# A layer-norm, linear-attention and gated-FFN block: apply order, folded query weights, and the first FFN handover

## The chip, the cores and the metric

The kernel runs on one core of a Trainium2 chip. The time is device microseconds from one launch; the median of 12 runs is compared. A core has five engines that work from queues of their own and wait for each other through semaphores: TensorE (PE, matmuls; PEld is its weight load), VectorE (DVE), ScalarE (ACT), GpSimd (POOL) and SyncE (SP, which here only issues DMAs).

## The reference, cut to what matters

With S = 2048 rows, D = 640, H = 32 heads of Dh = 20, FF = 1536, all in bfloat16:

```python
def _A_ref(x, wqkv, w_phi, wo):                     # x is layernorm(A_x)
    qkv = (x @ wqkv).reshape(B, S, 3, H, Dh)...     # q, k, v per head
    pq, pk = q @ w_phi[h], k @ w_phi[h]             # per head, Dh x Dh
    phi_q = concat([softmax(pq), softmax(-pq)])
    phi_k = concat([softmax(pk), softmax(-pk)])
    kv, z = phi_k^T v, sum_s phi_k                  # over all rows
    o = (phi_q kv) / (phi_q z + 1e-6)
    return o.reshape(B, S, D) @ wo
def _B_ref(x, w_gate, w_up, w_down):
    return (gelu(x @ w_gate) * (x @ w_up)) @ w_down
h  = x + _A_ref(layernorm(x), ...)
h2 = h + _B_ref(layernorm(h), ...)
```

## The kernel before, in words

The rows are cut into NT = 16 tiles of 128 rows, in NB = 4 blocks of four tiles; D is NC = 5 chunks of 128. All five engines run in the order in which the program issues their instructions: the whole body stands under a manual schedule, so nothing is reordered, and an instruction that waits holds everything behind it on its engine.

**Stage 1, the k/v loop.** `w_phi` is folded into the key and query weights (`fold`, L203): for each of five row chunks d, six matmuls into one PSUM tile `wa`, copied to `Wk2` or `Wq2` by ACT (L212, even d) or DVE (L214, odd d). Layer norm of a tile has two steps. `ln_st` takes the statistics of two tiles at a time: on DVE `stats` (L101) and `mv` (L102), on POOL `ve` (L104), `rstd` (L106) and `mr` (L111). `ln_ap` applies them on ACT (L117), and SP issues a DMA transpose into `LN1T` (L133); the first six tiles use TensorE transposes instead. The loop over t = 0 to 15 does `k_tile(t)` (ten matmuls L239 into `pk`, and two exponentials `E` on ACT, L262), `v_tile(t+3)` (ten matmuls into `pv`, and a copy `vS` on ACT, L250), `ln_ap(t+5)`, at odd t `ln_st(t+7, t+8)`, then `k_norm(t)` and, at odd t from 5 on, `kv_tile(t-5)` and `kv_tile(t-4)` (40 matmuls together, L284). `k_norm` is on DVE a sum per head `sk` (L268) and a reciprocal `rs` (L270), and then two products `vt` (L273): one half always on POOL, the other on POOL for odd t up to 11 and on DVE otherwise. At t = 1 POOL also fills `KV` and `kmask` (L353 to L361). At t = 12 the whole query fold runs, ahead of `v_tile(15)`. At t = 10 SP issues the loads of `Wo` and `Wu`.

**Stage 2, the query features.** There are 20 chunks (4 blocks by 5 chunks of D). `q_mm(j)` computes chunks 2j and 2j+1 into one PSUM tile `pq` (ten matmuls of 512 columns, L307), and `q_exp(j)` takes exp of both signs on ACT into `Eq[j]` (L312). Groups 0 to 3 run after t = 15 and ahead of the last `kv_tile`s (tiles 12 to 15) and of `kv_mask`, which makes `KV`; groups 4 to 9 are laid between the attention steps of tiles 0 and 1.

**Stage 3, attention, and handover to the FFN.** Per tile: `attn_a` (20 matmuls into two PSUM tiles `ab`, and two copies to `AB`, L412), `attn_b`, `b2`, `b3` (products, reciprocal, `tt` L441, `o` L445), a transpose into `oT`, `attn_c` (ten matmuls `po`, L460), `attn_d` (residual add L469 and statistics), `attn_e` (apply and transpose into `LN2T`). For tiles 0 and 1 the sequence is written out by hand. The FFN then starts with `gate_up` on columns 0 to 256 of block 0 (L500; `g` on ACT L503, `GT` on DVE L506), and `weave` lays the other tiles' attention steps between FFN units by position numbers.

**PSUM.** `gtile` hands out tiles of two banks in rotation: three of them in stages 1 and 2 (`psG`; `kvp` has the other two banks), four from group 4 on (`psG2`). A matmul that opens a tile waits until the tile handed out three (or four) requests ago has been read. So the order of the requests decides which ACT or DVE instruction a matmul waits for:

```python
psG = ps_cm.enter_context(tc.tile_pool(name="psG", bufs=3, space=PSUM, reuse_waits="tile"))
psG = ctx.enter_context(tc.tile_pool(name="psG2", bufs=4, space=PSUM, reuse_waits="tile"))
```

Of the kernel before, what the change touches and what calls it, by code (L numbers as in the profile page):

```python
# [8 lines left out]
BF16 = mybir.dt.bfloat16  # L9
F32 = mybir.dt.float32  # L10
ALU = mybir.AluOpType
ACTF = mybir.ActivationFunctionType
# [5 lines left out]
def kernel(  # L18
# [12 lines left out]
    nc = tc.nc  # L31
    P = 128
# [5 lines left out]
    NT = S // P  # L38
# [7 lines left out]
    NH = [(P * c + P - 1) // Dh - H0[c] + 1 for c in range(NC)]  # L46
    NWARM = 10
    VP = (1, 3, 5, 7, 9, 11)
    QT = (15, 15, 15, 15)
    VC = Dh + 1  # L50
    KC = Dh + 2
# [22 lines left out]
    Wu = const.tile([P, NC, FF], BF16, name="Wu")  # L74
    KV = const.tile([P, NC, 2, 4, KC], BF16, name="KV")

    Eq = [const.tile([P, 2, 2, 512], BF16, name=f"Eq{j}") for j in range(NB * NC // 2)]
    ident = const.tile([P, P], BF16, name="ident")
    hmask = const.tile([P, NC, 8], BF16, name="hmask")
    kmask = const.tile([P, NC, 4], BF16, name="kmask")  # L80
# [1 line left out]
    nhalf = const.tile([P, 2], F32, name="nhalf")  # L82

    def eq(t, c, s):
        j = t // 4 * NC + c
        return Eq[j // 2][:, j % 2, s, t % 4 * P:(t % 4 + 1) * P]

    def small(pool, shape, name, bufs=3):
        return pool.tile(shape, F32, name=name, bufs=bufs)
# [1 line left out]
    def gtile(name):  # L91
        return psG.tile([P, 2, 512], F32, name=name, tag="G")
# [93 lines left out]

    warm(NWARM)

    def fold(WT, W2, halves):


        runs = []
        for c in range(NC):
            lo, hi = H0[c] * Dh, (H0[c] + NH[c]) * Dh
            for u in range(2):
                a, b = max(lo, u * HD), min(hi, (u + 1) * HD)
                if a < b:
                    runs.append((u, c, a, b))
        runs.sort()
        for d in range(NC):  # L200
            wa = gtile("wa")
            for i, (u, c, a, b) in enumerate(runs):
                nc.tensor.matmul(wa[:, u, a - u * HD:b - u * HD], lhsT=WT[:, c, d * P:(d + 1) * P],  # L203
                                 rhs=BD[:, c].rearrange("p a b -> p (a b)")[:, a - H0[c] * Dh:b - H0[c] * Dh],
                                 start=(i == 0 or runs[i - 1][0] != u),
                                 stop=(i + 1 == len(runs) or runs[i + 1][0] != u), skip_group_check=True)
            dst, src = W2[:, d, :].rearrange("p (u f) -> p u f", u=2), wa[:, :, 0:HD]
            if halves:
                dst = W2[:, d, :].rearrange("p (c u f) -> p u c f", c=NC, u=2)
                src = src.rearrange("p u (c f) -> p u c f", c=NC)  # L210
            if d % 2 == 0:
                nc.scalar.copy(dst, src)  # L212
            else:
                nc.vector.tensor_copy(dst, src)  # L214
# [3 lines left out]
    def ln_st(*tiles, act=True):  # L218
        for t, v in zip(tiles, ln_stats(p1, [x_sb[t // 4][:, t % 4, :] for t in tiles], "1", act)):
            lnp[t] = v  # L220

    def ln_ap(t, on_act=False, on_pe=False):
        ln = (ln_act if on_act else ln_dve)(p1, "1", *lnp[t])
        if on_pe:
            lnp[t] = ln
        else:
            transpose_to(LN1T[t // 4][:, :, t % 4 * P:(t % 4 + 1) * P], ln, False)

    def ln_tp(t):
        transpose_to(LN1T[t // 4][:, :, t % 4 * P:(t % 4 + 1) * P], lnp[t], True)  # L230
# [22 lines left out]
    def v_tile(t):  # L253
        v_mm(t)
        v_ev(t)

    def k_tile(t):
        pk = gtile("pk")
        proj(pk, t, Wk2)
        Ek[t] = ev.tile([P, 2, D], BF16, name="E", bufs=8)  # L260
        for s in range(2):
            nc.scalar.activation(Ek[t][:, s, :].rearrange("p (u f) -> p u f", u=2), pk[:, :, 0:HD],  # L262
                                 ACTF.Exp, scale=(1.0 if s == 0 else -1.0))

    def k_norm(t):

        sk = small(p1, [P, 2 * H], "sk")
        nc.vector.reduce_sum(sk, Ek[t].rearrange("p s (h f) -> p (s h) f", f=Dh), axis=AX.X)  # L268
        rs = small(p1, [P, 2 * H], "rs")
        nc.vector.reciprocal(rs, sk)  # L270
        vt = ev.tile([P, 2, H, VC], BF16, name="vt", bufs=8)
        for s, eng in ((1, nc.gpsimd), (0, nc.gpsimd if t in VP else nc.vector)):
            eng.tensor_tensor(vt[:, s], vS[t % 6], rs[:, s * H:(s + 1) * H, None].to_broadcast([P, H, VC]), ALU.mult)  # L273
        Vt[t] = vt
# [3 lines left out]
    def kv_tile(t):  # L278

        for s in range(2):  # L280
            for c in range(NC):
                for u in range(2):
                    f0, h0 = u * HD + c * 64, u * UH + 3 * c
                    nc.tensor.matmul(kvp[HALF[u], s, c * 4 * VC:(c + 1) * 4 * VC],  # L284
                                     lhsT=Ek[t][:, s, f0:f0 + 64], rhs=Vt[t][:, s, h0:h0 + 4, :],
                                     start=(c == 0 and t == 0), stop=(t == NT - 1), skip_group_check=True)
# [10 lines left out]

    pqs = {}

    def q_mm(j, i=None):  # L300

        if i != 1:
            pqs[j] = gtile("pq")
        for i in range(2) if i is None else (i,):
            b, c = divmod(2 * j + i, NC)
            for kc in range(NC):
                nc.tensor.matmul(pqs[j][:, i, :], lhsT=Wq2[:, kc, c * P:(c + 1) * P], rhs=LN1T[b][:, kc, :],  # L307
                                 start=(kc == 0), stop=(kc == NC - 1))

    def q_exp(j, signs=(0, 1)):  # L310
        for s in signs:
            nc.scalar.activation(Eq[j][:, :, s, :], pqs[j], ACTF.Exp, scale=(1.0, -1.0)[s])  # L312

    ln_st(0, act=False)
    ln_st(1, act=False)
# [26 lines left out]
    ev = ev_cm.__enter__()  # L342

    for t in range(NT):
        k_tile(t)
        if t == 0:
            ln_ap(4, on_pe=True)
            ln_tp(4)
            ln_ap(5, on_pe=True)
            ln_st(6, 7)  # L350
        if t == 1:
            ln_tp(5)
            nc.gpsimd.memset(KV, 0.0)  # L353
            nc.gpsimd.memset(kmask, 1.0)
            for r in HALF:
                nc.gpsimd.affine_select(out=kmask[r], in_=kmask[r], pattern=[[4, NC], [-Dh, 4]],
                                        compare_op=ALU.is_ge, fill=0.0, base=0, channel_multiplier=1)
                nc.gpsimd.affine_select(out=kmask[r], in_=kmask[r], pattern=[[-4, NC], [Dh, 4]],
                                        compare_op=ALU.is_ge, fill=0.0, base=Dh - 1, channel_multiplier=-1)
            nc.gpsimd.tensor_copy(KV[:, :, 0, :, KC - 1], kmask)  # L360
            nc.gpsimd.tensor_copy(KV[:, :, 1, :, 0], kmask)  # L361
        if t == 12:
            fold(WqT, Wq2, True)
        if t + 3 < NT:
            v_tile(t + 3)
        if 6 <= t + 5 < NT:
            ln_ap(t + 5, on_act=True)
        if t % 2 == 1 and t + 7 < NT:
            ln_st(t + 7, t + 8)
        k_norm(t)  # L370
        if t % 2 == 1 and t >= 5:
            kv_tile(t - 5)
            kv_tile(t - 4)
        if t == 10:
            nc.sync.dma_start(Wo, wo_v)
            nc.sync.dma_start(Wu, wu_v)
        for j in range(len(QT)):
            if t == QT[j]:
                q_mm(j)
                q_exp(j)  # L380
# [14 lines left out]

    LN2T, st = {}, {}

    def attn_a(t, dve=False):

        b = t // 4  # L400
        if b not in LN2T:
            LN2T[b] = p2.tile([P, NC, 512], BF16, name="LN2T", bufs=2)
        AB = p2r.tile([P, 2, H, KC], F32, name="AB", bufs=2)
        ab = gtile("ab"), gtile("ab")
        for s in range(2):
            for c in range(NC):
                for u, r in enumerate(HALF):
                    nc.tensor.matmul(ab[u][:, s, 3 * c * KC:(3 * c + 4) * KC], lhsT=eq(t, c, s)[r],  # L408
                                     rhs=KV[r, c, s].rearrange("p h f -> p (h f)"),
                                     start=(c == 0), stop=(c == NC - 1), skip_group_check=True)  # L410
        for u in range(2):
            (nc.vector.tensor_copy if dve and u == 1 else nc.scalar.copy)(  # L412
                AB[:, :, u * UH:(u + 1) * UH].rearrange("p s h f -> p s (h f)"), ab[u][:, :, 0:UH * KC])
        st[t] = AB

    def attn_b(t, on_pe=False):

# [59 lines left out]
    def attn_d2(t):  # L477
# [10 lines left out]
        nc.gpsimd.tensor_scalar(v[:, 2:3], sm[:, 0:1], rstd, -1.0 / D, op0=ALU.mult, op1=ALU.mult)  # L488
        st[t] = ht, None, rstd, v[:, 2:3]

    def attn_e(t, on_pe=False, on_dve=False):
        ln = (ln_dve if on_pe else ln_act)(p2, "2", *st[t])
        transpose_to(LN2T[t // 4][:, :, t % 4 * P:(t % 4 + 1) * P], ln, on_pe, on_dve)

    def gate_up(b, f, a0, a1):
# [58 lines left out]


    q_mm(q)
    attn_a(0, True)
    q_exp(q)
    q_mm(q + 1)
    attn_b(0, True)  # L560
    attn_b2(0, True)
    attn_b3(0, True)
    attn_a(1, True)
    q_exp(q + 1)
    q_mm(q + 2)
    attn_t(0)
# [8 lines left out]
    attn_t(1)  # L575
    q_exp(q + 3, (1,))
    q_mm(q + 4)
    attn_c(1)
    q_exp(q + 4)
    q_mm(q + 5, 0)  # L580
    attn_e(0, True)
    attn_d(1, False)
    q_mm(q + 5, 1)
    q_exp(q + 5)
    attn_a(2)
    attn_e(1, True, True)
    assert q + 6 == len(Eq)

    def attn_at(t, i, offs):

# [48 lines left out]
```

## Time and profile before

| what | value |
|---|---|
| median of 12 runs | 289.67 us (288.59 to 290.19) |
| the profiled execution's own time | 288.59 us |
| its span, first to last instruction | 286.9 us, so 1.7 us lie around it |
| TensorE busy | 274.0 us (96%), granted clock 0.999 |
| TensorE weight load busy | 172.2 us (60%) |
| DVE, ACT, POOL busy | 167.9, 143.8, 98.0 us |

Busy shares of TensorE count pipelined matmuls, whose ends are modelled, so a row of ten projections shows 1.52 us but follows the row before it after 1.36 us. Times within the span are starts in microseconds from its beginning. In a row of the timeline the first number is the start, the second the length; the bracket at the end is how long the engine had been idle before, and what ended that.

### The profile page before, as it was taken

What the parts mean: (1) busy time and instruction counts of PE and PEld (TensorE: products, weight loads), DVE (VectorE), ACT (ScalarE), POOL (GpSimd) and SP (SyncE); (2) the same over time, 40 slices, a digit from 0 to 9 for tenths busy, and PEclk for the clock granted to TensorE, in tenths of its full rate; (3) what the DMA queues carried; (4) which work ended last, traced back from release to release, by engine and by line L of the source; (5) the groups of instructions that cost most, each with busy time, mean ns of one, the idle gap of its engine ahead of it and who ended that gap; (6) DMA issues with size and microseconds to landing.
All of it is one profiled execution on the core that took longest, in us unless ns stands there. A gap on an engine that the chain in (4) does not pass through costs nothing.

```text
span 286.9 us, 5742 instructions
## 1 busy us (share of the span) xinstructions
PE 274.0 (96%) x2314; PEld 172.2 (60%) x2329; DVE 167.9 (59%) x284; ACT 143.8 (50%) x228; POOL 98.0 (34%) x209
## 2 busy tenths in 40 slices
PE   7899899979999899999999999999999999999995
PEld 2676577755545577777874454676455567444573
DVE  6789999989268466675623657532485732323322
ACT  2578788665968867536425445332445441132200
POOL 6239977866210223643420246220124340000000
PEclk9999999999999999999999999999999999999999
DMA  7997422390080011323311112232021323000011
GB/s 229 250 341 214 49 47 49 61 375 4 2 276 0 0 20 30 56 62 70 69 30 42 23 23 49 47 66 73 0 44 23 52 46 93 25 1 0 0 48 46
DMA packets 40971, 21.05 MB, mean 73 GB/s; under 512 B 33136, under 2 KB 39280, under 8 KB 40944
## 3 DMA queue, kind: packets, MB, share of 16 engines
q1 hardware_dynamic: 39856, 19.67, 27.2%
q10 hardware_dynamic: 1088, 1.01, 1.1%
q8 instruction: 18, 0.29, 0.4%
q14 instruction: 9, 0.07, 0.1%
HBM read 10.18 MB, written 2.62 MB: 45 GB/s over the span
## 4 chain that ended last, share of the span: by engine, by line
PE 74%; DVE 15%; DMA 3%; ACT 3%; issue 1%; POOL 1%; SPq 0%; DVEq 0%; ACTq 0%; POOLq 0%
PE gu L500 34%; PE pd L515 18%; PE pq L307 8%; PE po L460 7%; DVE sk L268 6%; DVE vt L273 3%; DMA Wv<-in_A_wqkv_dram 2%; DVE rs L270 2%; PE ab L408 2%; DVE stats L101 2%; PE pk L239 2%; PE pv L239 2%; ACT Eq L312 1%; DMA oT<-o 1%; PE kvp L284 1%
## 5 line engine op out<-in xcount | busy, mean ns | idle before, releaser
L503 ACT ACTIVATE g<-gu 128x512 bf16<-128x512 f32 (+1 forms) x60 | 30.7, 512 | 73.5 <-PE gu L500 72.7
L506 DVE TENSOR_TENSOR GT<-gu,g 128x512 bf16<-128x512 f32 (+1 forms) x60 | 34.5, 581 | 55.9 <-ACT g L503 55.8
L500 PE MATMUL gu<-LN2T,Wg 128*128 128x512 bf16 (+1 forms) x289 | 61.3, 335 | 2.0 <-DVE GT L506 0.8
L500 PE MATMUL gu<-LN2T,Wu 128*128 128x512 bf16 (+1 forms) x300 | 61.7, 336 | 0.0
L515 PE MATMUL pd<-Wd,GT 128*128 128x320 bf16 x384 | 53.9, 299 | 0.0
L515 PEld LDWEIGHTS <-GT 128*128 128x128 bf16 x384 | 37.4, 98 | 15.7 <-DVE GT L506 0.9
L500 PEld LDWEIGHTS <-Wu 128*128 128x128 bf16 x300 | 29.4, 98 | 22.6
L500 PEld LDWEIGHTS <-Wg 128*128 128x128 bf16 x300 | 28.4, 98 | 22.3 <-issue 1.7
L239 PEld LDWEIGHTS <-LN1T 128*128 128x128 bf16 x320 | 30.5, 98 | 15.6 <-DMA LN1T<-ln 2.7
L273 POOL TENSOR_TENSOR vt<-vS,rs 128x672 bf16<-128x672 bf16 x22 | 34.5, 1591 | 8.9 <-DVE rs L270 7.3
L521 DVE TENSOR_TENSOR y<-pd,x_sb 128x640 bf16<-128x640 f32 (+1 forms) x17 | 13.3, 784 | 30.7 <-PE pd L515 30.7
L412 ACT COPY AB<-ab 128x704 f32<-128x704 f32 x30 | 21.0, 749 | 14.8 <-PE ab L408 14.5
L239 PE MATMUL pv<-Wv,LN1T 128*128 128x320 bf16 x160 | 24.2, 299 | 2.6 <-DMA LN1T<-ln 2.1
L460 PE MATMUL po<-Wo,oT 128*128 128x320 bf16 x160 | 24.4, 299 | 0.2 <-DMA oT<-o 0.2
L239 PE MATMUL pk<-Wk,LN1T 128*128 128x320 bf16 x160 | 24.2, 299 | 0.3 <-DVE Wk L214 0.3
L441 DVE TENSOR_TENSOR tt<-AB,w 128x1280 bf16<-128x1280 f32 x16 | 23.8, 1486 | 1.2 <-POOL w L434 0.9
L262 ACT ACTIVATE E<-pk 128x640 bf16<-128x640 f32 x32 | 20.7, 702 | 7.1 <-PE pk L239 7.0
L268 DVE TENSOR_REDUCE sk<-E 128x64 f32<-128x1280 bf16 x16 | 23.2, 1452 | 0.8 <-ACT E L262 0.8
L307 PE MATMUL pq<-LN1T,Wq 128*128 128x512 bf16 x96 | 22.7, 379 | 0.6 <-ACT Eq L312 0.4
L312 ACT ACTIVATE Eq<-pq 128x1024 bf16<-128x1024 f32 x20 | 19.4, 1025 | 3.4 <-PE pq L307 3.4
L460 PEld LDWEIGHTS <-oT 128*128 128x128 bf16 x160 | 15.5, 98 | 7.6 <-DMA oT<-o 0.6
L483 POOL TENSOR_SCALAR v<-sm 128x1 f32<-128x1 f32 x14 | 8.4, 602 | 30.3 <-DVE x_sb L474 30.3
(77 smaller groups left out, 259.1 us busy)
## 6 DMA issues: line engine op xcount, KB each, us to landing
out_dram<-y SPq DMA_DIRECT2D x15, 160.0 KB, 1.8
Wg<-in_B_w_gate_dram SPq DMA_DIRECT2D x1, 1920.0 KB, 10.9
Wu<-in_B_w_up_dram SPq DMA_DIRECT2D x1, 1920.0 KB, 9.5
Wd<-in_B_w_down_dram SPq DMA_DIRECT2D x1, 1920.0 KB, 7.9
x_sb<-in_A_x_dram SPq DMA_DIRECT2D x2, 640.0 KB, 5.8
Wv<-in_A_wqkv_dram SPq DMA_DIRECT2D x2, 400.0 KB, 7.2
Wo<-in_A_wo_dram SPq DMA_DIRECT2D x1, 800.0 KB, 5.3
x_sb<-in_A_x_dram ACTq DMA_DIRECT2D x1, 640.0 KB, 7.3
```

What stands on the lines that cost most here:

```text
L239: nc.tensor.matmul(ps[:, u, 0:HD], lhsT=lnT(t, c), rhs=W[:, c, u * HD:(u + 1) * HD], start=(c == 0), stop=(c == NC - 1))
L268: nc.vector.reduce_sum(sk, Ek[t].rearrange("p s (h f) -> p (s h) f", f=Dh), axis=AX.X)
L273: eng.tensor_tensor(vt[:, s], vS[t % 6], rs[:, s * H:(s + 1) * H, None].to_broadcast([P, H, VC]), ALU.mult)
L307: nc.tensor.matmul(pqs[j][:, i, :], lhsT=Wq2[:, kc, c * P:(c + 1) * P], rhs=LN1T[b][:, kc, :], start=(kc == 0), stop=(kc == NC - 1))
L312: nc.scalar.activation(Eq[j][:, :, s, :], pqs[j], ACTF.Exp, scale=(1.0, -1.0)[s])
L412: (nc.vector.tensor_copy if dve and u == 1 else nc.scalar.copy)(AB[:, :, u * UH:(u + 1) * UH].rearrange("p s h f -> p s (h f)"), ab[u][:, ...
L441: nc.vector.tensor_tensor(tt.rearrange("p s (h f) -> p s h f", f=Dh), num, w[:, :, :, None].to_broadcast([P, 2, H, Dh]), ALU.mult)
L460: nc.tensor.matmul(po[:, u, 0:HD], lhsT=st[t][:, c, :], rhs=Wo[:, c, u * HD:(u + 1) * HD], start=(c == 0), stop=(c == NC - 1))
L500: nc.tensor.matmul(gu[:, i, 0:n], lhsT=W[:, c, f * P:(f + 1) * P], rhs=LN2T[b][:, c, a0:a1], start=(c == 0), stop=(c == NC - 1))
L503: nc.scalar.activation(g[:, 0:n], gu[:, 0, 0:n], ACTF.Gelu_apprx_tanh)
L506: nc.vector.tensor_tensor(st[b, "g", f][:, a0:a1], gu[:, 1, 0:n], g[:, 0:n], ALU.mult)
L515: nc.tensor.matmul(pd[:, u, 0:HD], lhsT=st[b, "g", f][:, tl * P:(tl + 1) * P], rhs=Wd[:, f, u * HD:(u + 1) * HD], start=(f == 0), stop=(f ...
```

## The change

Three places in the program are edited.

1. In the k/v loop `ln_ap(t+5)` is issued ahead of `k_tile(t)` instead of after `v_tile(t+3)`. The query fold is cut into its five pieces, one each at t = 8 to 12, after `v_tile` and ahead of `k_norm`. POOL's filling of `KV` and `kmask` goes from t = 1 to the end of t = 9.
2. The query chunks are grouped by the table `QG`: eleven groups in place of ten, of two chunks but for chunks 6 and 15, which stand alone. The four groups ahead of the last `kv_tile`s hold 7 chunks instead of 8; 13 follow.
3. In the hand-written sequence for tiles 0 and 1, `attn_e` is split so that the apply (`attn_ln`) can stand apart from the transpose. The last groups are not cut in halves any more, the copy of tile 0's `LN2T` goes from ACT to DVE, and `attn_a(2)` goes behind tile 1's transpose, with both its copies on DVE instead of ACT.

```diff
+    FQ = (8, 9, 10, 11, 12)
+    QG = ((0, 1), (2, 3), (4, 5), (6,), (7, 8), (9, 10), (11, 12), (13, 14), (15,), (16, 17), (18, 19))
...
-    Eq = [const.tile([P, 2, 2, 512], BF16, name=f"Eq{j}") for j in range(NB * NC // 2)]
+    Eq = [const.tile([P, len(g), 2, 512], BF16, name=f"Eq{j}") for j, g in enumerate(QG)]
...
-    def fold(WT, W2, halves):
+    def fold(WT, W2, halves, ds=range(NC)):
...
-        for d in range(NC):
+        for d in ds:
...
+    def q_mm(j):
+        pqs[j] = gtile("pq")
+        for i, bc in enumerate(QG[j]):
+            b, c = divmod(bc, NC)
...
-            nc.scalar.activation(Eq[j][:, :, s, :], pqs[j], ACTF.Exp, scale=(1.0, -1.0)[s])
+            nc.scalar.activation(Eq[j][:, :, s, :], pqs[j][:, 0:len(QG[j])], ACTF.Exp, scale=(1.0, -1.0)[s])
...
     for t in range(NT):
+        if 6 <= t + 5 < NT:
+            ln_ap(t + 5, on_act=True)
         k_tile(t)
...
         if t == 1:
             ln_tp(5)
+        if t + 3 < NT:
+            v_tile(t + 3)
+        if t % 2 == 1 and t + 7 < NT:
+            ln_st(t + 7, t + 8)
+        if t in FQ:
+            fold(WqT, Wq2, True, [FQ.index(t)])
+        k_norm(t)
+        if t % 2 == 1 and t >= 5:
+            kv_tile(t - 5)
+            kv_tile(t - 4)
+        if t == 9:
             nc.gpsimd.memset(KV, 0.0)
             nc.gpsimd.memset(kmask, 1.0)
...
-        if t == 12:
-            fold(WqT, Wq2, True)
-        if t + 3 < NT:
-            v_tile(t + 3)
-        if 6 <= t + 5 < NT:
-            ln_ap(t + 5, on_act=True)
-        if t % 2 == 1 and t + 7 < NT:
-            ln_st(t + 7, t + 8)
-        k_norm(t)
-        if t % 2 == 1 and t >= 5:
-            kv_tile(t - 5)
-            kv_tile(t - 4)
...
-    def attn_a(t, dve=False):
+    def attn_a_mm(t):
...
+    def attn_a_ev(t, dve=0):
+        AB, ab = st[t]
         for u in range(2):
-            (nc.vector.tensor_copy if dve and u == 1 else nc.scalar.copy)(
+            (nc.vector.tensor_copy if u >= 2 - dve else nc.scalar.copy)(
                 AB[:, :, u * UH:(u + 1) * UH].rearrange("p s h f -> p s (h f)"), ab[u][:, :, 0:UH * KC])
...
+    def attn_a(t, dve=0):
+        attn_a_mm(t)
+        attn_a_ev(t, dve)
...
+    def attn_ln(t, on_pe=False):
+        st[t] = (ln_dve if on_pe else ln_act)(p2, "2", *st[t])
+
     def attn_e(t, on_pe=False, on_dve=False):
-        ln = (ln_dve if on_pe else ln_act)(p2, "2", *st[t])
+        if not on_pe:
+            attn_ln(t)
+        ln = st[t]
...
     q_mm(q + 4)
+    q_exp(q + 4)
     attn_c(1)
-    q_exp(q + 4)
-    q_mm(q + 5, 0)
-    attn_e(0, True)
+    q_mm(q + 5)
+    q_exp(q + 5)
+    attn_ln(0, True)
     attn_d(1, False)
-    q_mm(q + 5, 1)
-    q_exp(q + 5)
-    attn_a(2)
+    attn_e(0, True, True)
+    q_mm(q + 6)
+    q_exp(q + 6)
+    attn_ln(1, True)
     attn_e(1, True, True)
-    assert q + 6 == len(Eq)
+    attn_a(2, 2)
+    assert q + 7 == len(Eq)
```

More of the change, by code (lines that the diff above doesn't have):

```diff
@@ L84, in eq @@
     def eq(t, c, s):
-        j = t // 4 * NC + c
-        return Eq[j // 2][:, j % 2, s, t % 4 * P:(t % 4 + 1) * P]
+        for E, g in zip(Eq, QG):
+            if t // 4 * NC + c in g:
+                return E[:, g.index(t // 4 * NC + c), s, t % 4 * P:(t % 4 + 1) * P]
     def small(pool, shape, name, bufs=3):
@@ L298 @@
     pqs = {}
[L300 to L305, printed above, removed]
+    def q_mm(j):
+        pqs[j] = gtile("pq")
+        for i, bc in enumerate(QG[j]):
+            b, c = divmod(bc, NC)
             for kc in range(NC):
@@ L410, in attn_a @@
                                      start=(c == 0), stop=(c == NC - 1), skip_group_check=True)
+        st[t] = AB, ab
+    def attn_a_ev(t, dve=0):
+        AB, ab = st[t]
         for u in range(2):
-            (nc.vector.tensor_copy if dve and u == 1 else nc.scalar.copy)(
+            (nc.vector.tensor_copy if u >= 2 - dve else nc.scalar.copy)(
                 AB[:, :, u * UH:(u + 1) * UH].rearrange("p s h f -> p s (h f)"), ab[u][:, :, 0:UH * KC])
         st[t] = AB
+    def attn_a(t, dve=0):
+        attn_a_mm(t)
+        attn_a_ev(t, dve)
     def attn_b(t, on_pe=False):
@@ L556 @@
     q_mm(q)
-    attn_a(0, True)
+    attn_a(0, 1)
     q_exp(q)
@@ L562 @@
     attn_b3(0, True)
-    attn_a(1, True)
+    attn_a(1, 1)
     q_exp(q + 1)
```

## The prediction, made before the changed kernel was run

> **What bounds the kernel now.** I read the engine shares, the chain that ended last, the timeline of TensorE (PE) for its gaps, and then the timeline of all engines around each gap.
>
> ```profile
> PE 274.0 (96%) x2314; PEld 172.2 (60%) x2329; DVE 167.9 (59%) x284; ACT 143.8 (50%) x228; POOL 98.0 (34%) x209
> PEclk9999999999999999999999999999999999999999
> ...
> PE 74%; DVE 15%; DMA 3%; ACT 3%; issue 1%; POOL 1%; SPq 0%; DVEq 0%; ACTq 0%; POOLq 0%
> ```
>
> PE is busy 96% of the span at full granted clock, and 74% of the chain is PE; the other large part is DVE (15%), all of it before 60 us. On the Trainium skill, "Perfetto Trace Analysis", Identifying the Most-Contended Engine, matmul busy time is a poor measure of headroom and weight-load busy time a good one. By it (60%) 40% of the span, some 115 us, would be open. The rows speak otherwise: ten projections follow each other in 1.36 us, forty `pq` matmuls in 8.66 us (67.98 to 76.64), without a gap between. I go by the gaps, which is all that an order can win:
>
> ```profile
> 26.93 1.53 PE L239 MATMUL pv<-Wv,LN1T 128*128 128x320 bf16 x10 [0.65 <-DMA LN1T<-ln]
> ...
> 33.94 1.53 PE L239 MATMUL pv<-Wv,LN1T 128*128 128x320 bf16 x10 [1.40 <-DMA LN1T<-ln]
> ...
> 58.48 0.47 PE L203 MATMUL wa<-BD,WqT 128*128 128x140 bf16 x6 [0.76 <-ACT E L262]
> ...
> 59.05 0.76 DVE L214 CAST Wq<-wa 128x640 bf16<-128x640 f32 x1
> ...
> 59.87 0.79 PE L203 MATMUL wa<-BD,WqT 128*128 128x140 bf16 x12 [0.91 <-DVE Wq L214]
> ...
> 97.94 0.45 PE L130 MATMUL tp<-ident,ln 128*128 128x128 bf16 x5 [0.62 <-DVE ln L122]
> ...
> 98.97 0.71 PE L500 MATMUL gu<-LN2T,Wg 128*128 128x256 bf16 x5 [0.58 <-DVE LN2T L131]
> ```
>
> The bracket is the idle time. PE waits for a transposed tile (`LN1T`) at 26.9 and 33.9 us; from the end of the matmuls before, this is 0.81 and 1.57 us (24.76 + 1.36 and 31.01 + 1.36 to the next start). The query fold waits for `E` and for its DVE copies (0.75 and 0.92 us): the copies at 59.05 stand on DVE behind the `k_norm`s. Group 4 waits 0.38 us for `Eq`. At the handover PE idles 0.62, 0.58 and 0.37 us (at 97.9, 99.0, 102.3). That is 6 us in all, 4.4 of it ahead of attention. From 102.3 us on there are only 0.5 us (130.4) and 0.4 us (141.9).
>
> ```profile
> 38.56 0.21 DVE L102 BATCH_NORM_AGGREGATE mv<-stats 128x2 f32<-128x12 f32 x1
> ...
> 39.98 0.50 POOL L111 TENSOR_SCALAR mr<-mv,rstd 128x1 f32<-128x1 f32 x2
> ...
> 40.69 1.29 ACT L262 ACTIVATE E<-pk 128x640 bf16<-128x640 f32 x2
> ...
> 42.57 0.92 ACT L117 ACTIVATE ln<-x_sb,mr,rstd 128x640 bf16<-128x640 bf16 x1
> ...
> 47.41 0.50 POOL L111 TENSOR_SCALAR mr<-mv,rstd 128x1 f32<-128x1 f32 x2
> ...
> 50.31 1.28 DVE L273 TENSOR_TENSOR vt<-vS,rs 128x672 bf16<-128x672 bf16 x1
> ```
>
> The third view is the cover of the change's first step: what the apply needs. At t = 7 the statistics end on DVE at 38.77, POOL gives `mr` at 40.2, `E` of t = 7 starts on ACT at 40.69, and the apply only at 42.57. So the apply never waits for `mr` today. DVE has hardly a gap from 18.9 to 51.6 us (the timeline lists none above 0.2 us); `mr` cannot come earlier.
>
> **The change part by part.** I walk the queues with the trace's spacings: projection 1.36 us; fold piece 0.40 (0.79 for two at 56.9); pair of `kv_tile`s 0.98 (41.74 to 42.72); query chunk 1.08 (8.66/8); on ACT apply to `E` 0.82, two `E` 1.30, `E` to `vS` 1.19, `vS` to the next 0.59; `Wq` copy 0.69 on ACT, 0.79 on DVE.
>
> *Apply ahead of `k_tile`.* Same instructions; the SP order of transposes, and of `Wo`/`Wu` behind them, is unchanged. The apply of tile 6 runs at 20.3 instead of 22.95 and its transpose lands before 25 (3.0 us later; 3.9 for tile 8), so both `LN1T` waits go. The price is that `E(t)` stands behind the apply. At t = 1 this costs PE 0.4 us (E ends 22.4, `pk(2)` needs its buffer). Then pv(8) starts at 32.0 instead of 33.94. Moving POOL's filling away lets `mr` of tiles 8 and 9 come at 25.6 instead of 27.26, in time.
>
> *The new wait.* At t = 5, 7, 9 the apply waits for `mr` of the statistics two steps back: 32.8, 40.2, 47.7 us by the rows. Behind it on ACT are `E(t)`, `vS` and, from t = 8, a `Wq` copy; on them wait `pk`/`pv` through the three PSUM tiles. The walk: t = 5, hidden (PE reaches its next need of that tile at 35.7, E ends 35.0). t = 7: E ends 42.4, pv(11) could open at 42.1: 0.3 us. From t = 8 the fold piece takes one request in three, so `pk(t+1)` opens the tile that `E(t)` has to free: `pk(9)` waits 0.8 us (E(8) ends 44.97), `pk(10)` 0.7 us (E(9) ends 49.84). Nothing in the trace shows this wait. Below it is 0 (if ACT or PE arrive later than walked, the wait is already paid); above, 0.82 plus 1.30 us for each of the three, 6.4 us. I take the walk's 1.9, since every term is a row; both ends are kept.
>
> *Fold in pieces.* The PE work (2.0 us) and five copies stay; the waits of 0.75 and 0.92 us go. DVE's two copies now sit after `vt(8)` (ends 51.6, so 52.4) and after `vt(10)` (58.7); the pieces that need their tiles come at 52.6 and 59.85: 0.2 and 1.2 us of cover. If DVE were late, PE would stall one for one.
>
> *POOL filling.* 2.5 us (23.02 to 25.54) go behind `vt(9)`, to 57.5 to 60. Behind it are `vt(10)` and `vt(11)`, done by 64.5; `kv_tile`(10, 11) asks at 65.3: covered by 0.8 us. A rule speaks against this: the Trainium skill, "SBUF — State Buffer", SBUF: two separate sides, has DVE operations with two inputs and POOL exclude each other for a whole instruction. The rows with a collision show DVE's `vt` at 1.35 instead of 0.86 us. At t = 1 the filling slowed nothing on DVE (`sk` 1.43 there and elsewhere); at its new place it meets `vt(10)` at most. By the row 0, by the rule 0.5 us on DVE, inside the 1.2 us of cover: 0 on the sum either way.
>
> *Seven chunks ahead of KV.* PE then runs pk(12) at 57.1, pv(15), fold, pk(13), kv at 61.6, pk(14), pk(15), kv at 65.3, queries from 66.3 to 73.8, last `kv_tile`s to 75.5. DVE, later by two copies and earlier by its old gaps, ends `vt(15)` at 73.1 and POOL's half at 74.2; tile 15 is asked for at 75.1: covered. Group 4 waits for the one-chunk exponentials (not in the trace: between half of 1025 ns and 597 ns, the FFN's 128x512 row; I take 0.55) until 75.9. `attn_a(0)` starts at 78.2 instead of 80.99: 2.8 us, less the 1.08 us of the chunk put off, **1.7 us won**.
>
> *Handover.* In the old frame: `pq` of one chunk ends at 91.95 instead of 93.02, but `attn_c(1)` opens the tile of group 7, whose second exponential ends at 92.51 (it stands behind the `oT` copy): 0.55 us of new idling. Then group 9, transpose 0, group 10 (to 98.6), transpose 1, `attn_a(2)`, 99.4. The first FFN unit needs `LN2T` (99.5) and the tile of group 10, so its exponentials, 98.7 to 100.65. The activation table load (1.28 us) now follows at once instead of after ACT's two `AB` copies, which move to DVE (0.89 instead of 0.75 us each; idle there, GT waits 2.9 us today). First `g` at 101.95 for 101.40, third FFN unit at 103.4. Less the chunk, 102.3 against 102.29: **0**. The waits inside this stage are from -0.6 us (no idling at `attn_c(1)`) to +0.6 us.
>
> Sum: -1.7 us and 0. Against the profiled execution's own 288.59 us (span 286.9) that is 286.9 us; that run is the lowest of the twelve, 1.1 us under the median, so against the median 289.67 it is **287.9 us**.
>
> One more rule weighs on the new stalls: the Trainium skill, "TensorE: Matmul & The Clock Gate", A second HAM failure mode, has short idles between groups that rotate through PSUM drop the clock. Here the granted clock is 9 of 10 or more in all 40 slices, after stalls of 0.81 and 1.57 us too, so I charge 0. By the rule, a half clock over the 8 us of matmuls between 42 and 50 us would cost 4 us at most (an estimate), and the sum turns to +2.3.
>
> **The rivals.**
> (a) *The new wait costs nothing*: PE's stalls at t = 7 to 9 do not appear. For it: each is only 0.3 to 0.8 us, of spacing errors added over 20 us. Against it: `mr` is paced by DVE, which is full. Then -1.7 - 1.9 = -3.6, 286.1 us.
> (b) *The loop wins, the handover gives back*: `attn_c(1)` and the first FFN unit idle by 0.6 us more each. For it: both wait for ACT, which is 4.97 of 5 us busy between 85 and 90. -0.5, 289.2 us.
> (c) *Slower: the statistics pace the loop.* The place is the apply at t = 5, 7 and 9; the price is up to 2.1 us each. The edit wins 0.81 + 1.57 + 0.75 + 0.92 = 4.05 us of old waits less 0.4 at t = 1; it turns slower once the three waits take over 3.6 us together, 1.2 each. With 1.5 each it is +0.9, 290.6 us. Against: POOL had been idle 0.95 us ahead of each `ve`.
> (d) That the change does not do what it says: the orders are the program's own, so I give it nothing.
>
> **How the numbers follow.** The walk 0.57 (own range 287.0 to 288.8), (a) 0.21, (b) 0.15, (c) 0.07. Changes within 0.2% (0.58 us) are about what a measurement of this kernel cannot tell from none. Faster: 0.57 + 0.21 + nearly half of (b) = 0.85; same 0.08; slower 0.07. The range 285.9 to 289.6 takes in the walk, (a) and most of (b), and leaves (c) out.
>
> **What would show it.** Right: no PE wait on `LN1T`; `pv(8)` near 32 us; ACT idling for POOL's `mr` ahead of the applies of tiles 10, 12, 14; PE waiting on ACT's `E` at 42 to 50 us; no wait on `Wq`; first `ab` matmul near 78.2; then `po` waiting about 0.5 us on `Eq`, and the first `gu` on the last `Eq`. Wrong: `wa` waiting on DVE, `kvp` waiting on `vt`, or a granted clock under 0.99.

## The result, and the profile after

The changed kernel takes 286.13 us (median of 8 runs, 285.38 to 287.14) against 289.55 us before (32 runs); the ratio is 0.9882, 95% interval 0.9864 to 0.9901. It is faster by 3.4 us, twice the 1.7 us of the walk and close to what rival (a) had, though not for its reason.

The two profiled executions must be compared with care. That of before (288.59 us) was the fastest of its first twelve; that of the changed kernel took 287.22 us, more than all eight other runs of it. In the changed kernel's profile the start was late, ahead of all edited code: TensorE waited 1.1 us for `Wv` and 0.8 us for the key weights' transpose `WkT` (before: 0.6 us and nothing), and the first `pk` matmul started at 17.42 us instead of 16.05. So stretches are counted from the first `pk`; the rows shown keep the start that the profile gives. From the page of the changed kernel, engine shares, clock row and chain:

```profile
PE 273.5 (96%) x2314; PEld 172.1 (60%) x2329; DVE 170.6 (60%) x287; ACT 141.7 (50%) x227; POOL 97.2 (34%) x209
...
PEclk9999999999999999999999999999999999999999
...
PE 77%; DVE 9%; DMA 6%; ACT 3%; POOL 2%; issue 2%; DVEq 0%; ACTq 0%; POOLq 0%
```

Shares and clock are as they were; in the chain DVE fell from 15% to 9%, PE rose from 74% to 77%. The rows of the timeline of TensorE and ACT that answer to the gaps shown of before (the bracket is the idle time ahead of the row's first instruction):

```profile
17.42 1.52 PE L243 MATMUL pk<-Wk,LN1T 128*128 128x320 bf16 x10 [0.18 <-DVE Wk L218]
...
28.75 1.53 PE L243 MATMUL pv<-Wv,LN1T 128*128 128x320 bf16 x10 [0.73 <-DMA LN1T<-ln]
...
34.19 1.52 PE L243 MATMUL pv<-Wv,LN1T 128*128 128x320 bf16 x10
...
46.55 1.52 PE L243 MATMUL pk<-Wk,LN1T 128*128 128x320 bf16 x10 [0.39 <-ACT E L266]
...
49.30 0.92 ACT L121 ACTIVATE ln<-x_sb,mr,rstd 128x640 bf16<-128x640 bf16 x1 [1.62 <-POOL mr L115]
...
51.46 1.52 PE L243 MATMUL pk<-Wk,LN1T 128*128 128x320 bf16 x10 [0.83 <-ACT E L266]
...
54.17 0.48 PE L207 MATMUL wa<-BD,WqT 128*128 128x140 bf16 x6
...
61.23 0.48 PE L207 MATMUL wa<-BD,WqT 128*128 128x140 bf16 x6
```

None of the five fold pieces has a bracket, the two shown and the three others: no wait for DVE's copies is left. The wait at pv(8), 1.40 us before, is gone, but that at pv(6) is still there. Two waits for `E` are new (0.39 and 0.83 us; a third, 0.21 us at pk(2), is the price at t = 1, walked at 0.4). The ACT row shows what is behind the second, an apply that keeps ACT waiting 1.62 us for `mr`. The same kernel at the handover, all engines:

```profile
79.17 0.57 PE L412 MATMUL ab<-KV,Eq 64*128 64x88 bf16 x20
...
88.79 0.83 DVE L481 TENSOR_TENSOR x_sb<-po,x_sb 128x640 bf16<-128x640 f32 x1 [0.37 <-PE po L472]
...
89.66 2.01 ACT L315 ACTIVATE Eq<-pq 128x1024 bf16<-128x1024 f32 x3
...
89.95 1.52 PE L472 MATMUL po<-Wo,oT 128*128 128x320 bf16 x10
...
95.90 0.44 PE L134 MATMUL tp<-ident,ln 128*128 128x128 bf16 x5
96.10 1.94 ACT L315 ACTIVATE Eq<-pq 128x1024 bf16<-128x1024 f32 x2 [0.50 <-PE pq L310]
...
96.39 0.49 DVE L135 COPY LN2T<-tp 128x640 bf16<-128x640 bf16 x1 [0.71 <-PE tp L134]
...
96.88 1.69 DVE L420 COPY AB<-ab 128x704 f32<-128x704 f32 x2
96.93 0.71 PE L517 MATMUL gu<-LN2T,Wg 128*128 128x256 bf16 x5
...
98.06 1.28 ACT L520 ACT_TABLE_LOAD   x1
...
100.25 0.71 PE L517 MATMUL gu<-LN2T,Wg 128*128 128x256 bf16 x5 [0.37 <-DVE GT L523]
```

`po` of tile 1 and the first `gu` have no bracket either: they start at 89.95 and 96.93 while ACT is still working on exponentials that the prediction had them wait for (to 90.7 and to 98.0 us; the row at 89.66 holds group 7's second exponential, which takes 1.03 us, and the two of group 8). The same three places in the timeline of before:

```profile
16.05 1.52 PE L239 MATMUL pk<-Wk,LN1T 128*128 128x320 bf16 x10 [0.29 <-DVE Wk L214]
...
80.99 0.56 PE L408 MATMUL ab<-KV,Eq 64*128 64x88 bf16 x20
...
102.29 0.71 PE L500 MATMUL gu<-LN2T,Wg 128*128 128x256 bf16 x5 [0.37 <-DVE GT L506]
```

This table, from these rows, splits the gain:

| | first pk to first ab | less a chunk (1.08) put off | first ab to third gu | chunks in it |
|---|---|---|---|---|
| before | 64.94 us | | 21.30 us | 10 |
| changed | 61.75 us | 62.83 us | 21.08 us | 11 |

The loop wins 64.94 - 62.83 = 2.1 us (predicted 1.7), the handover 21.30 - (21.08 - 1.08) = 1.3 us (predicted 0). Behind the third `gu` nothing was edited, and single profiles differ there without regard to the edits: 184.6 to 185.4 us to the end in the four kernels with the old handover, 184.5 to 185.2 us in the eight with the new one (before 184.6, changed 185.2). So the two profiles differ by 2.8 us from the first `pk` to the end; that 2.1 and 1.3 add up to just the 3.4 us of the medians is more exact than they can show.

### The profile page after: what moved, and what is told of

Read it like the earlier page. It is cut to its first block, busy times and chain, and to the rows that moved or that the text cites. A ratio compares the mean times of both kernels' runs of the same rounds, so it can differ in the third digit from the quotient of the medians.

```text
span 285.5 us, 5745 instructions
## 1 busy us (share of the span) xinstructions
PE 273.5 (96%) x2314; PEld 172.1 (60%) x2329; DVE 170.6 (60%) x287; ACT 141.7 (50%) x227; POOL 97.2 (34%) x209
## 4 chain that ended last, share of the span: by engine, by line
PE 77%; DVE 9%; DMA 6%; ACT 3%; POOL 2%; issue 2%; DVEq 0%; ACTq 0%; POOLq 0%
PE gu L517 34%; PE pd L532 18%; PE pq L310 8%; PE po L472 7%; DMA WkT<-in_A_wqkv_dram 4%; PE pk L243 4%; DVE sk L272 3%; PE ab L412 2%; DVE stats L105 2%; PE kvp L288 2%; PE pv L243 1%; POOL vt L277 1%; DVE vt L277 1%; DMA oT<-o 1%; DVE rs L274 1%
## 5 line engine op out<-in xcount | busy, mean ns | idle before, releaser
L420 ACT COPY AB<-ab 128x704 f32<-128x704 f32 x28 | 19.6, 748 | 14.4 <-PE ab L412 14.1
L315 ACT ACTIVATE Eq<-pq 128x1024 bf16<-128x1024 f32 (+1 forms) x22 | 19.4, 950 | 4.7 <-PE pq L310 4.7
```

Of the source, the lines that this page charges most:

```text
L420: (nc.vector.tensor_copy if u >= 2 - dve else nc.scalar.copy)(AB[:, :, u * UH:(u + 1) * UH].rearrange("p s h f -> p s (h f)"), ab[u][:, :, ...
```

## The experiments

**Which half wins.** Two kernels cut the change in two.

`e1_groups_handover`, the changed kernel with the old loop:

```diff
     for t in range(NT):
-        if 6 <= t + 5 < NT: ln_ap(t + 5, on_act=True)
         k_tile(t)
...
+        if t == 12: fold(WqT, Wq2, True)
...
+        if 6 <= t + 5 < NT: ln_ap(t + 5, on_act=True)
...
-        if t in FQ: fold(WqT, Wq2, True, [FQ.index(t)])
```

> The loop of before with the new query groups and the new handover. Walk of the prediction (PSUM tiles in strict rotation): 0 against before, 289.5 us. Theory now (a tile request gets the tile whose last read was issued earliest, so attn_c(1) and the first FFN unit do not wait for exponentials): 1.3 us faster, near 288.2 us, and from the first ab matmul to the third FFN unit about 21.1 us for 11 chunks, against 21.3 us for 10 before.

`e2_loop`, the kernel before with the new loop:

```diff
-    for t in range(NT): ...      # old loop
+    for t in range(NT): ...      # loop of the changed kernel; groups, Eq and handover as before
```

> The new k/v loop (apply ahead, fold in pieces, POOL filling at t = 9) with the old query groups and the old handover. Walk of the prediction: 1.7 us faster, 287.8 us. Theory now, from the two profiles counted from the first pk matmul: 2.1 us faster, 287.4 us. If the loop had won all 3.4 us, it would be 286.1 us and the handover nothing.

Measured: the groups and handover alone 287.88 us, ratio 0.9927 (0.9903 to 0.9952); the loop alone 287.89 us, ratio 0.9932 (0.9914 to 0.9950). Each wins about 1.9 us against 289.74 us of the kernel before, and 1.86 + 1.85 is 3.7 us, the whole within the noise. Counted from the first `pk`, the first `ab` comes 62.8 us later with the new loop (before: 64.9). With the old loop and a chunk less it comes 80.24 - 16.50 = 63.7 us later: nothing is won there but the chunk. First `ab` to third `gu` takes 101.33 - 80.24 = 21.09 us with the new handover, 21.30 us with the old one. So the walk of the loop held, and the handover's zero was wrong.

**Why the handover's zero was wrong.** `e3_after_rotation` and `e4_before_rotation` force on stage 3 what the walk had assumed, four PSUM tiles in strict turn:

```diff
+    strict = []
     def gtile(name):
-        return psG.tile([P, 2, 512], F32, name=name, tag="G")
+        if not strict:
+            return psG.tile([P, 2, 512], F32, name=name, tag="G")
+        strict[0] += 1
+        return psG.tile([P, 2, 512], F32, name=name, tag=f"G{strict[0] % 4}")
...     # the tile `tp` of a transpose takes its tag from the same count
-    psG = ...(name="psG2", bufs=4, space=PSUM, reuse_waits="tile")
+    psG = ...(name="psG2", bufs=1, space=PSUM, reuse_waits="tile")
+    strict.append(-1)
```

> The changed kernel with the four PSUM tiles of stage 3 handed out in strict rotation by four tags, as the prediction had assumed. Theory (order of release was the error): po of tile 1 waits about 0.5 us for the exponentials of group 7, the first gu waits over 1 us for those of the last group, and the time is about 1.3 us above the changed kernel, 287.4 us. Rival (the handover won because the AB copies left ACT, whatever tile is handed out): within 0.3 us of the changed kernel, 286.1 us.

> The kernel before with the same strict rotation, as a control. By the rotation the transpose of tile 1 opens the tile of the last query group and waits 0.9 us for its exponentials: 0.9 us above before, 290.4 us. If the handing out does not matter: 289.5 us.

Measured: 290.49 us for the changed kernel with rotation (ratio to before 1.0028, 1.0013 to 1.0042), 4.4 us above the changed kernel; 293.26 us for the old one (ratio 1.0116, 1.0077 to 1.0155), 3.5 us above before. (Three of the six runs of the old one had a mean granted clock of 0.99 instead of 1.00; the other three have a median of 292.5 us, 2.8 us above before.) TensorE in the first of them, and the last group's exponentials on ACT:

```profile
81.97 0.57 PE L420 MATMUL ab<-KV,Eq 64*128 64x88 bf16 x20 [0.46 <-ACT Eq L322]
...
85.20 0.44 PE L141 MATMUL tp<-ident,o 128*128 128x128 bf16 x5 [0.39 <-ACT Eq L322]
...
91.14 1.52 PE L480 MATMUL po<-Wo,oT 128*128 128x320 bf16 x10 [0.63 <-ACT Eq L322]
...
97.29 1.94 ACT L322 ACTIVATE Eq<-pq 128x1024 bf16<-128x1024 f32 x2 [0.50 <-PE pq L317]
...
99.28 0.70 PE L525 MATMUL gu<-LN2T,Wg 128*128 128x256 bf16 x5 [1.25 <-ACT Eq L322]
```

Both waits of the walk are there, on `Eq`, and of its size: 0.63 us at `po` (walk 0.55) and 1.25 us at the first `gu` (walk 1.2). In the changed kernel they don't exist. That is shown: the pool does not hand tiles out in turn. The waits in the two built programs bear it out. In the changed kernel `po` of tile 1 opens the tile that tile 0's residual add has read, and the first `gu` the tile that the copy of tile 1's `LN2T` has read; both reads are DVE's, and the rows above show them over at 89.62 and 96.88 us, just ahead of `po` and `gu`. Under rotation both wait for ACT's `Eq`. In both cases the pool gave the tile that was free earlier in time. It is not the order of the program's text: there the last group's `q_exp` stands ahead of that copy of `LN2T`, and yet its tile, read until 98.04 us, went to the `ab` that starts at 98.11 us. By what rule the pool estimates when a tile is free is not shown here. The rival, that only the copies' move to DVE counts, is out. The price was larger than expected for a reason also in these rows: under rotation the second `ab` and a transpose wait too (0.46 and 0.39 us). First `ab` to third `gu` takes 23.4 us instead of 21.1; the other 2 us of the 4.4 come later in the FFN, where two `po` wait under rotation that don't wait in the changed kernel, 0.8 us for `GT` and 1.0 us for `y`, the read of a tile of `down`. In the old kernel under rotation tile 1's transpose waits 1.53 us for `Eq` (expected 0.9).

**Is the new wait on the path?** `e5_late_apply`, `e6_wg_later` and `e7_both` edit the changed kernel:

```diff
# e5_late_apply
-        if 6 <= t + 5 < NT:
+        if 6 <= t + 5 < NT and t not in (5, 7, 9):
             ln_ap(t + 5, on_act=True)
         k_tile(t)
+        if t in (5, 7, 9): ln_ap(t + 5, on_act=True)
# e6_wg_later
-    for dst, src in (..., (x_sb[3], x_v[:, 12:16, :]), (Wg, wg_v)):
+    for dst, src in (..., (x_sb[3], x_v[:, 12:16, :])):
...
             nc.sync.dma_start(Wo, wo_v)
+            nc.sync.dma_start(Wg, wg_v)
# e7_both: both
```

> The changed kernel (286.1 us) with the apply behind k_tile again at t = 5, 7 and 9 alone, the three steps at which it waits for POOL's mr. Theory (the new wait lies on the path): pk(9) and pk(10) lose their 0.4 and 0.8 us for E, 1.2 us faster, 284.9 us. Rival (DVE paces the loop anyway): the idle time comes back as a wait for Wq or for vt, 286.1 us.

> The changed kernel (286.1 us) with the load of Wg issued at t = 10, beside Wo and Wu, instead of ahead of the loop. Theory: the first transpose of the loop took 6.1 us to land since Wg was under way; it then lands in about 2.6 us and pv(6) does not wait (0.7 to 0.9 us in the changed kernel); but the waits for E at pk(9) and pk(10) grow by as much, since mr is paced by DVE: 286.1 us, 0.3 us less at most. Rival (the wait at pv(6) is on the path): 285.2 us.

> The changed kernel with both edits, the late apply at t = 5, 7, 9 and Wg at t = 10. Theory: with the wait for mr gone the earlier pv(6) counts too: 1.2 + 0.9 = 2.1 us faster, 284.0 us, unless DVE's vt of the last tiles then stops the last kv_tiles (its margin there was 0.6 us). Rival (DVE paces): 286.1 us.

Measured: 286.26 us (ratio to before 0.9904, 0.9870 to 0.9938), 286.60 us (0.9888, 0.9870 to 0.9906) and 286.22 us (0.9882, 0.9864 to 0.9899): none can be told from the changed kernel. The single waits went away as expected. The late apply took both waits for `E`, the later `Wg` took the wait at pv(6) (longest landing of an `LN1T` transpose 4.2 us instead of 6.1) and left three for `E` in its place (0.38, 0.76 and 0.82 us). But with the late apply PE waits for the DVE copy of the second fold piece, 0.43 us (and at pv(6) 1.43 us), and with both edits 1.67 us, nearly all that they had freed:

```profile
52.98 0.81 DVE L218 CAST Wq<-wa 128x640 bf16<-128x640 f32 x1
...
53.85 0.48 PE L207 MATMUL wa<-BD,WqT 128*128 128x140 bf16 x6 [1.67 <-DVE Wq L218]
```

The idle time moved. From the first `pk` to the first `ab` the brackets of TensorE add up to 2.2 us in the changed kernel and to 2.1, 2.2 and 1.9 us in these three, and the stretch is as long as it was (61.75 us; 61.60, 61.75 and 61.61 us). DVE paces PE here, through `mr` or through `Wq`: whichever wait is taken away, the next one ends at another instruction of DVE's queue. The expectations that 1.2 or 2.1 us would come were wrong, their rival right; that of `e6_wg_later` held but for its size (286.60 us, where at most 286.1 us had been expected).

**Which edit of the loop counts.** `e8_apply_only` and `e9_fold_only` do one edit each on the kernel before, the second together with POOL's filling at t = 9:

```diff
# e8_apply_only
     for t in range(NT):
+        if 6 <= t + 5 < NT: ln_ap(t + 5, on_act=True)
         k_tile(t)
...
             v_tile(t + 3)
-        if 6 <= t + 5 < NT: ln_ap(t + 5, on_act=True)
# e9_fold_only: in the kernel of e2_loop
     for t in range(NT):
-        if 6 <= t + 5 < NT: ln_ap(t + 5, on_act=True)
         k_tile(t)
...
             v_tile(t + 3)
+        if 6 <= t + 5 < NT: ln_ap(t + 5, on_act=True)
```

> The kernel before (289.7 us) with the apply ahead of k_tile and nothing else. By single gaps one would count 2 us (the LN1T waits of 0.81 and 1.57 us less 0.4). Theory: the fold at t = 12 still waits for DVE copies that DVE reaches at 59 us whatever PE does, so PE waits there for longer and the time stays 289.7 us within 0.3 us. Rival: the early waits are on the path, 287.7 us.

> The loop of before with the fold in pieces (and POOL's filling at t = 9), the apply at its old place behind v_tile, old query groups and old handover. Theory: it is the fold that carries the loop's gain, since its copies no longer stand at the end of DVE's queue of k_norms; PE has its LN1T waits still, but they are hidden by DVE's pace: the same as the whole new loop, 287.8 us, 62.8 us from the first pk to the first ab matmul (before 64.9). Rival: both edits are needed, and this is near 289.0 us.

Measured: the apply alone 291.07 us, ratio 1.0049 (1.0033 to 1.0065), which is slower; the fold 287.81 us, ratio 0.9927 (0.9904 to 0.9950), as fast as the whole new loop, and 62.96 us from the first `pk` to the first `ab`. So the fold in pieces, with the filling behind it, carries all the loop's gain, and the apply ahead adds nothing measurable to it; what the filling does alone was not run. By itself the apply lets PE reach the old fold earlier and wait there longer, as expected; what was not expected is the 1.4 us lost. The figure mixes two kinds of run. Each run has its mean granted clock on record: eight of the 22 were at full clock, with a median of 289.75 us, the 289.7 us that had been expected; fourteen were at 0.993 or 0.994, with a median of 291.7 us (290.4 to 292.4). The 27 runs of before beside them were all at full clock. The profile is one of the fourteen. Fold and projection in its timeline, and the windows of the same stretch (PE, PEld, DVE, ACT, POOL busy, then the granted clock, DMA):

```profile
58.16 0.48 PE L203 MATMUL wa<-BD,WqT 128*128 128x140 bf16 x6 [0.76 <-ACT E L262]
...
59.45 0.76 DVE L214 CAST Wq<-wa 128x640 bf16<-128x640 f32 x1
...
60.26 1.36 PE L203 MATMUL wa<-BD,WqT 128*128 128x140 bf16 x12 [1.63 <-DVE Wq L214]
...
61.41 2.48 PE L239 MATMUL pv<-Wv,LN1T 128*128 128x320 bf16 x10
```

```profile
58.00:60.00 2.00, 0.48 (x6) 0.35 (x6) 1.90 (x3) 1.36 (x3) 0.98 (x2) 0.99 1.04 412
60.00:61.00 1.00, 0.74 (x8) 0.74 (x8) 0.21 (x1) 0.00 (x0) 1.00 (x2) 0.50 1.03 402
61.00:62.00 1.00, 1.00 (x10) 0.76 (x8) 0.94 (x2) 0.35 (x1) 1.00 (x1) 0.50 0.80 310
62.00:63.00 1.00, 1.00 (x5) 0.54 (x4) 1.00 (x1) 0.35 (x1) 0.27 (x1) 0.50 0.04 15
63.00:64.00 1.00, 1.00 (x7) 0.68 (x6) 0.86 (x3) 0.02 (x1) 0.00 (x0) 0.82 0.00 0
64.00:65.00 1.00, 1.00 (x10) 0.69 (x7) 0.82 (x1) 0.68 (x1) 0.90 (x1) 1.00 0.00 0
```

PE does 0.48 us of matmuls in 2.9 us (0.76 and 1.63 us idle around them), and then its granted clock is 0.50 for more than 3 us: ten projections take 2.48 us on the row instead of 1.52, twelve fold matmuls 1.36 instead of 0.79. In the profile of before the same two waits, 0.76 and 0.91 us, left the clock at 1.00:

```profile
58.00:60.00 2.00, 0.60 (x9) 0.48 (x9) 1.72 (x3) 1.69 (x3) 0.98 (x2) 1.00 1.07 395
60.00:61.00 1.00, 1.00 (x16) 0.89 (x15) 0.62 (x1) 0.30 (x1) 1.00 (x2) 1.00 1.04 421
```

Three us at half clock and one at 0.82 cost 1.7 us (an estimate from these rows), about the 1.9 us between the two kinds of run. So the loss is the clock's. Before is not quite free of it: one of its 40 runs beside `e1_groups_handover` (292.46 us) and one of nine beside `e12_final` (290.55 us) were at 0.994 too.

**A faster version.** Since DVE paces the loop, `e10_all` takes its two fold copies away too and puts the pieces at t = 10 to 14, where ACT has an apply at the first only; `e11_fold_act` does only this; `e12_final` puts the apply ahead of `k_tile` only for t = 1 to 4:

```diff
# e11_fold_act, on the changed kernel
-    FQ = (8, 9, 10, 11, 12)
+    FQ = (10, 11, 12, 13, 14)
-            if d % 2 == 0:
+            if d % 2 == 0 or halves:
                 nc.scalar.copy(dst, src)
# e10_all: this, and the edits of e7_both
# e12_final: this, Wg at t = 10, and
-        if 6 <= t + 5 < NT: ln_ap(t + 5, on_act=True)
+        if 1 <= t < 5: ln_ap(t + 5, on_act=True)
         k_tile(t)
...
             v_tile(t + 3)
+        if 5 <= t < NT - 5: ln_ap(t + 5, on_act=True)
```

> The changed kernel with the late apply at t = 5, 7, 9, Wg at t = 10, and the fold pieces at t = 10 to 14 with all five copies on ACT, so that no matmul waits for DVE in the loop. If DVE's Wq copies are what paced PE in the kernel with both earlier edits (1.67 us of waiting), PE has no wait from the first pk matmul to the queries: 59.5 us to the first ab matmul instead of 61.75, about 284.0 us. Rival: DVE's k_norms pace it still through the last kv_tiles, which then wait for vt; 285.5 us or more.

> The changed kernel with only the fold moved: pieces at t = 10 to 14, all five copies on ACT; apply and Wg as in the changed kernel. Theory: with no fold piece at t = 8 and 9 the PSUM tile that E frees is asked for later, so the waits at pk(9) and pk(10) shrink by about 0.5 us each, and no wait for DVE comes in their place: 285.2 us. Rival: mr paces E all the same, 286.1 us.

> The kernel of e10_all with the apply ahead of k_tile only at t = 1 to 4, and behind v_tile, as before the change, from t = 5 on. In e10_all ACT still idled 1.66 us for mr at t = 9 with vS and the next E behind it, and pk waited 1.16 us. Theory: that wait goes and nothing takes its place, 284.4 us, 59.6 us from the first pk to the first ab matmul (60.7 in e10_all). Rival (DVE's pace): the last kv_tiles wait for vt of tile 15 and the time is that of e10_all, 285.5 us.

Measured: `e11_fold_act` 286.06 us (0.9875, 0.9852 to 0.9898), the changed kernel's time, so its rival held: PE still waited 0.50 and 0.75 us for `E`. `e10_all` 285.46 us (0.9850, 0.9827 to 0.9872), 60.7 us to the first `ab`, where 59.5 had been expected: at t = 9 the apply still waited 1.66 us for `mr`, with `vS` and the next `E` behind it; its interval overlaps that of the changed kernel (0.9864 to 0.9901). `e12_final` 284.91 us, ratio 0.9835 (0.9814 to 0.9857), 4.9 us under before and, by the ratios, 1.4 us under the changed kernel, with an interval apart from that one's. It missed its 284.4 us in part by what its rival had named:

```profile
72.38 1.99 POOL L277 TENSOR_TENSOR vt<-vS,rs 128x672 bf16<-128x672 bf16 x1 [1.03 <-DVE rs L274]
...
72.58 1.53 PE L288 MATMUL kvp<-vt,E 128*64 128x84 bf16 x70
74.42 0.38 PE L288 MATMUL kvp<-vt,E 128*64 128x84 bf16 x10 [0.31 <-POOL vt L277]
...
77.00 0.57 PE L415 MATMUL ab<-KV,Eq 64*128 64x88 bf16 x20
```

The last ten matmuls of the last `kv_tile` wait 0.31 us for POOL's `vt` of tile 15, the end of the chain of `k_norm`s; another 0.28 us are spent at 52.51 us, where a `pv` waits for `vS`. The first `ab` comes 60.4 us after the first `pk` (expected 59.6).

## Why the prediction was right or wrong, point by point

*The loop's sum, 1.7 us, held* (2.1 us by the profiles, 1.85 us alone in `e2_loop`). Moved to the first `pk` of before, pv(8) started at 32.8 us (predicted 32.0) and the first `ab` at 77.8 us (78.2). *The handover's 0 did not*: it was 1.3 us by the profiles, 1.9 us in `e1_groups_handover`, where the groups changed as well. The step that failed is the sentence that `attn_c(1)` opens the tile of group 7 and the first FFN unit that of group 10. Both rested on the reading, given in the section on the kernel too, that a request gets the tile handed out four requests ago. It got a tile that was free earlier: `po` of tile 1 the one that tile 0's residual add had read, and the first `gu` the one that the copy of tile 1's `LN2T` had read. The two waits, 0.55 and 1.2 us in the walk, are those that the rotation kernel shows (0.63 and 1.25) and the changed kernel lacks. They come to more than the 1.3 us won, since the last exponentials, the table load behind them (1.28 us at 98.06 us), `g` and `GT` still end in a wait of 0.37 us at the third `gu`. Rival (b) had the same two waits, larger by 0.6 us each, and fell with them. In the k/v loop the built program does hand the three tiles out in turn, so that the same assumption did no harm there.

*Both `LN1T` waits go*: half right. The one at pv(8) went; the one at pv(6) stayed (0.73 us), since the first transpose took 6.1 us to land, not 3.0. It was now issued while the 1.9 MB of `Wg` were under way; before, at 23.92, nearly all of that had passed (the DMA traffic fell from some 400 GB/s to under 250 at 24 us before, and at 26 us in the changed kernel). The walk had taken a landing time from a row issued later and moved it to where the queue was full. `e6_wg_later` shows that this cost nothing, since DVE paced what followed.

*The new wait*: the mechanism was right (ACT idled 0.54, 1.60 and 1.62 us for `mr` at t = 5, 7, 9), its size at PE 1.2 us instead of 1.9 (none at t = 7, 0.39 us at pk(9), 0.83 us at pk(10)). But its meaning was wrong: `e5_late_apply` and `e7_both` show that without it PE waits for DVE's `Wq` copy. Rival (a), which counted 1.9 us for its absence, named a gain that isn't there; that the total comes near its 286.1 us is chance.

*Fold, filling, seven chunks*: right. No `wa` waited for DVE, no `kvp` for `vt`. The edits were summed as if each removed its own waits; in truth the waits for `LN1T` (0.81 and 1.57 us) were worth nothing and those of the fold nearly all, as `e8_apply_only` and `e9_fold_only` show. That the loop's sum came near all the same is in part luck: the wait left at pv(6), 0.73 us, and the 0.7 us by which the new waits were smaller than walked cancel.

*The two rules.* Of the Trainium skill, "SBUF — State Buffer", SBUF: two separate sides, the exclusive pair: a DVE operation with two inputs in SBUF is kept apart only from POOL operations that read SBUF, and the one that starts later waits for the whole of the other. `vt(10)` took 1.41 us on DVE at its new place (58.07), as 1.34 before (55.75), where a `vt` that starts ahead of POOL's product takes 0.86 us (67.80). At both places it meets POOL's product of tile 9, not the filling. In the changed kernel that product ends at 58.76 us; `vt(10)`, had it waited so long, would end at 59.62 us, and it ended at 59.48. So the rows agree with the page to 0.14 us, and moving the filling cost nothing: its first `memset` took 0.83 us at both places. "TensorE: Matmul & The Clock Gate", A second HAM failure mode: in the changed kernel the granted clock stayed at 0.999, so charging 0 was right. In `e8_apply_only` the clock did fall in this very loop, but after one stretch of 2.9 us that was nearly idle and in fourteen of 22 runs; whether that is the case that the page means is not shown.

*Small misreadings.* DVE's part of the chain before is not all ahead of 60 us: some 4 of 43 us lie behind it. The half clock over 8 us of matmuls would have cost 8 us and not 4, if it lasted until they were done. The one-chunk exponentials, taken at 0.55 us, took 0.60 to 0.62 us. None of the three changes the sum.

## What to carry to other kernels

Before a wait on a buffer is put into a sum, find out which buffer a request really gets: the semaphore that the instruction waits for in the built program tells it without a run. A wait that a profile shows is worth its length only if the engine that it waits for isn't itself the pace; follow that engine's queue to the next meeting point before the gap is counted. Taking work off the pacing engine helped only once the waits on its other results were gone too: the two copies alone won nothing (286.06 us), with the late apply and the later `Wg` they won 0.7 us (not clear of the noise), and with the apply late from t = 5 on 1.4 us. Compare two single profiles from a point behind the start-up transfers, and split the runs of a kernel by granted clock before their median is explained.

## What the runs showed of the hardware that had not been expected

The granted TensorE clock fell to 0.50 for over 3 us after 2.9 us in which PE had worked 0.48 us, in a loop that otherwise ran at 1.00. It did not do so in every run: of the 22 runs of the apply alone, eight show a mean clock of 1.00 and the time of before (289.75 us), fourteen show 0.993 or 0.994 and 291.7 us. A transpose of one tile between SBUF places landed in 2.6 us in the median, and in 6.0 to 6.9 us when it was issued 5 to 6 us behind a load of 1.9 MB of weights. The first `pk` matmul started between 16.0 and 17.7 us over the fourteen profiles, a spread of 1.7 us, half the effect measured here.
